# Early instruction fetches, branch hints and one-time credits in a decode attention kernel that is bound by its loads

## The chip, the cores and the metric

One core of a Trainium2 chip. The metric is the device time of one execution in microseconds; the profile's span, from the first to the last instruction, is about 1.35 us shorter in the kernel before.

## The reference, cut to what matters

One token for two batch entries: layer norm, a query projection, attention of 32 query heads over 8 cached heads with 32,768 positions each, an output projection, and beside it a small gated MLP whose result multiplies the attention's.

```python
xn = _layernorm(x)                       # x: 2 x 1 x 512
q = xn @ wq                              # 32 heads of 128
scores = einsum("bhqd,bhkd->bhqk", q, k) * Dh ** -0.5
o = einsum("bhqk,bhkd->bhqd", softmax(scores), v)     # k, v: 2 x 8 x 32768 x 128, bf16
out = x + (o @ wo) * silu(B(xn))         # B: the MLP with w1..w4
```

K and V are 268 of the 280.5 MB that are read. There are sixteen groups (batch entry, cached head), each with 8.39 MB of K and 8.39 MB of V.

## The kernel before

Every engine has its own program. SyncE issues all large loads, VectorE transposes K, TensorE multiplies, ScalarE takes exponentials. The first load is put ahead of the entry barrier; TensorE's loop runs once per group.

```python
def begin(nc, ins):                       # the first load goes ahead of SyncE's barrier
    ...
    at = next(n for n, i in enumerate(entry) if i.engine == ins.engine and isinstance(i, mybir.InstDrain))
    blocks[0].instructions = entry[:at] + [ins] + entry[at:]
...
    def load(cache, dst, sems, m):        # K or V of group m
        if m < last:
            sp.dma_start(out=dst, in_=row_view(cache, *groups[m])).then_inc(sems[0], 16)
            sp.sem_inc(sems[1], 16)       # the second half is credited at once
        else:
            for c in range(NPART):
                load_half(cache, dst, sems, m, c)
...
    for m in range(1, NG):
        sp.wait_ge(p_k, m)                # TensorE's mark: K's buffer is free
        load_k(m)
        sp.wait_ge(p_o, m)                # TensorE's mark: V's buffer is free
        load_v(m)
    ...                                   # then wo in seven pieces, the last two of 128 KB
...
    with pe.Fori(0, NG):                  # some 310 instructions, 16 passes
        head_sums()
        take(pe, s_z)
        for i in range(NPART):
            for r in range(NR):
                ...                       # 4 matmuls: scores
            mark(s_tf)
            if i == 0:
                mark(p_k)
        take(pe, s_p)
        ...                               # 1 + 64 matmuls: values
        mm.then_inc(s_o, 1)
        mark(p_o)
    ...                                   # products with wo as its pieces land
```

TensorE's program has 662 instructions, VectorE's 165, SyncE's 92, ScalarE's 62.

The softmax here doesn't subtract the row's maximum and nothing guards it: scores larger than these inputs give would overflow.

## Time and profile before

| | before |
|---|---|
| time, median (first three runs) | 654.27 us |
| span of the profiled run | 653.1 us |
| read from HBM | 280.50 MB, 429 GB/s over the span |
| DMA engines | busy throughout (99.4% of sixteen engines' span, queue q1) |
| TensorE, VectorE busy | 59%, 53% |
| instruction fetches in the span | two of 16 KB, two of 8 KB |

The DMA engines are the bound. The last landing is followed by a short tail: four matmuls, two VectorE operations, the output DMA (650.42 to 653.1 us). The rest of the reading is in the prediction. How late each DMA engine is, no row of the page tells; but the trace has sixteen updates of its semaphore for every load of the large queue. I read each as the end of one engine's share; it fits that the last piece has two late updates (1.22 and 1.25 us) where the DMA share is 0.13, and 0.13 x 16 is two engines. Below, "lateness" is the last of these sixteen less the first.

### The profile page before, as it was taken

Reading aid. Unit: us, or ns where it says so; the run is one execution under the profiler, and the core shown is the slowest. Engines: PE = TensorE matmul, PEld = TensorE weight load, DVE = VectorE, ACT = ScalarE, POOL = GpSimd, SP = SyncE. Lnnn points to the kernel's source line nnn. Section 1 sums busy time; section 2 is a strip of 40 time slices with the busy share of each in tenths; the row PEclk is TensorE's granted clock in tenths of the full one; section 3 lists DMA queues with packets and bytes.
Section 4 is the critical chain, followed back from the end, with each engine's and each line's share of the span. In section 5 each row is a group of like instructions: output and inputs, shape, how many; then the busy total and the mean of one; then the engine's idle time right before and its main releaser. Section 6 shows DMA issues by size and latency. Waiting matters only on the chain. (4 is left out here: it accounts for less than half of the span.)

```text
span 653.1 us, 6541 instructions
## 1 busy us (share of the span) xinstructions
PE 387.9 (59%) x2406; PEld 157.4 (24%) x2438; DVE 346.0 (53%) x412; ACT 76.6 (12%) x184; POOL 7.7 (1%) x29
## 2 busy tenths in 40 slices
PE   0658294673828558293754829366383955728785
PEld 0223131221313222131321213123131322303322
DVE  4266191754809266391835719174481926539570
ACT  1320102001010200101020010202001020200100
POOL 3100000000000000000000000000000000000000
PEclk9769788786978968698796978869597886959797
DMA  9989999999999999999999999999999999999997
GB/s 386 482 388 448 447 446 402 441 441 446 405 441 441 446 401 446 441 446 397 450 441 446 401 446 441 450 425 417 450 441 429 413 450 441 446 397 444 420 446 297
DMA packets 6508, 280.56 MB, mean 430 GB/s; under 512 B 736, under 2 KB 1000, under 8 KB 1256
## 3 DMA queue, kind: packets, MB, share of 16 engines
q1 hardware_dynamic: 6492, 280.50, 99.4%
q8 instruction: 2, 0.03, 0.0%
q14 instruction: 2, 0.02, 0.0%
q10 hardware_dynamic: 12, 0.01, 0.0%
HBM read 280.50 MB, written 0.00 MB: 429 GB/s over the span
## 5 line engine op out<-in xcount | busy, mean ns | idle before, releaser
L573 PE MATMUL bank<-T,z 128*128 128x512 bf16 x992 | 273.2, 423 | 188.1 <-PEq L46 183.9
L500 DVE STREAM_TRANSPOSE T<-kbuf 128x1024 int32<-128x1024 int32 x256 | 290.8, 1206 | 129.4 <-DVEq L46 129.4
L573 PEld LDWEIGHTS bank<-T,z 128*128 128x128 bf16 x1024 | 97.7, 103 | 350.9 <-issue 273.5
L590 PE MATMUL bank<-vbuf,pt 128*16 128x512 bf16 x1024 | 72.4, 444 | 4.5 <-PEq L46 3.3
L477 ACT ACTIVATE ep<-bank 128x512 bf16<-128x512 f32 x32 | 19.1, 597 | 438.5 <-ACTq L46 438.5
L521 DVE RECIPROCAL rec<-bank 128x1 f32<-128x1 f32 (+1 forms) x17 | 2.9, 169 | 120.6 <-DVEq L46 120.6
L590 PEld LDWEIGHTS bank<-vbuf,pt 128*16 128x16 bf16 x1024 | 27.7, 101 | 41.2 <-issue 22.7
L509 DVE STREAM_TRANSPOSE pt<-ep 128x512 bf16<-128x512 bf16 x32 | 22.7, 708 | 22.1 <-DVEq L46 22.1
L555 PE MATMUL bank<-ob,sel_o 128*128 128x128 f32 x136 | 20.6, 297 | 16.4 <-PEq L46 16.4
L583 PE MATMUL bank<-ones_f,sm 128*128 128x1 f32 x32 | 5.9, 252 | 31.3 <-PEq L46 31.3
L555 PEld LDWEIGHTS bank<-ob,sel_o 128*128 128x128 f32 x136 | 17.7, 203 | 21.8 <-issue 21.8
L481 ACT COPY ob<-bank 128x512 f32<-128x512 f32 x16 | 9.4, 586 | 103.6 <-ACTq L46 103.6
L470 ACT ACT_TABLE_LOAD x16 | 20.5, 1283 | 0.3
L470 ACT COPY z<-qr 32x16 bf16 x64 | 12.9, 201 | 0.7
L583 PEld LDWEIGHTS bank<-ones_f,sm 128*128 128x128 f32 x32 | 5.0, 195 | 32.2 <-issue 32.2
L439 PE MATMUL bank<-vbuf,h_bf 128*32 128x512 bf16 x14 | 5.6, 586 | 5.6 <-DVE h_bf L436 5.6
L550 PE MATMUL bank<-ident 128*1 128x1 bf16 x64 | 8.4, 165 | 0.0
L550 PEld LDWEIGHTS bank<-ident 128*1 128x1 bf16 x64 | 4.0, 82 | 16.1 <-issue 14.4
L529 DVE TENSOR_REDUCE oA<-xm 128x128 f32 x16 | 5.9, 366 | 3.8 <-DVEq L46 3.8
L316 PE MATMUL bank<-ident,xn_bf 17*128 17x17 bf16 x4 | 0.3, 175 | 12.8 <-POOL x L307 12.8
L523 DVE SCALAR_TENSOR_TENSOR xm<-bank,rec,mask 128x128 f32<-128x128 f32 (+1 forms) x17 | 6.0, 351 | 2.5 <-DVEq L46 0.2
L477 ACT ACTIVATION_READ_ACCUMULATOR ep<-bank 128x1 f32 x32 | 6.4, 199 | 0.2
(75 smaller groups left out, 55.7 us busy)
## 6 DMA issues: line engine op xcount, KB each, us to landing
vbuf<-in_A_v_cache_dram SPq DMA_DIRECT2D x4, 4096.0 KB, 29.0
kbuf<-in_A_k_cache_dram SPq DMA_DIRECT2D x2, 4096.0 KB, 22.7
kbuf<-in_A_wq_dram SPq DMA_DIRECT2D x1, 4096.0 KB, 12.3
vbuf<-in_B_w_dram SPq DMA_DIRECT2D x2, 1792.0 KB, 17.0
kbuf<-in_A_wo_dram SPq DMA_DIRECT2D x3, 1024.0 KB, 34.3
kbuf<-in_A_wo_dram SPq DMA_DIRECT2D x1, 512.0 KB, 37.1
kbuf<-in_A_wo_dram SPq DMA_DIRECT2D x1, 256.0 KB, 37.3
kbuf<-in_A_wo_dram SPq DMA_DIRECT2D x2, 128.0 KB, 36.7
```

The lines of the kernel that those rows point to most:

```text
L470: i = act.copy(out=z[32 * j:32 * j + 32, :, :, c:c + rep], in_=qr[32 * j:32 * j + 32, :, :, bass.ds(m * rep, rep)],)
L477: act.activation(out=eps_[i][:, :], in_=sc[i][:, :], func=ACT.Exp, scale=inv_sqrt_dh, accum_out=rss[i][:, :]).then_inc(s_e, 1)
L481: act.copy(out=ob[:, :], in_=o[:, :]).then_inc(s_ob, 1)
L500: dve.transpose(out=Ts[(NR * i + r) % T_BUFS][:, :].rearrange("p (b t k) -> p t b k", b=NB, t=RT), in_=kt[:, r * W:(r + 1) * W].rearrange( ...
L509: dve.transpose(out=pts[h][:, :, :].rearrange("p r (t h) -> p t r h", h=rep), in_=eps_[i][:, :].rearrange("p (t r h) -> p t r h", r=NR, h= ...
L523: dve.scalar_tensor_tensor(out=xm[p0:, :, :], in0=oT[p0:, :].rearrange("p (w r) -> p w r", w=WL), scalar=rec[p0:, 0:1], in1=mask[p0:, :].u ...
L529: dve.tensor_reduce(out=dst, in_=xm[p0:, :, :].rearrange("p w r -> p r w"), axis=AX.X, op=ALU.add).then_inc(s_r, 1)
L550: pe.matmul(mark_ps, lhsT=ident[:, 0:1], rhs=ident[:, 0:1], start=True, stop=True).then_inc(sem, 1)
L555: mm = pe.matmul(oT, lhsT=sel_o[:, t, :, :, :].rearrange("p j h w -> p (j h w)"), rhs=ob[:, t * Dh:(t + 1) * Dh], start=(t == 0), stop=(t ...
L573: mm = pe.matmul(sc[i][:, :], lhsT=z[:, nb, e, zc:zc + 128], rhs=Tb[:, nb, :, e], start=(r == 0 and nb == 0 and e == 0), stop=(r == NR - 1 ...
L583: pe.matmul(S, lhsT=sms[1][:, :], rhs=ones_f[:, 0:1], start=True, stop=True)
L590: mm = pe.matmul(o[32 * j:32 * j + VT * rep, :], lhsT=pts[h][:, r, a * VT * rep:(a + 1) * VT * rep], rhs=vt[:, u * VT:(u + 1) * VT, :].rea ...
```

## The change

Its intent: program text should be fetched at the start and not in the middle of the stream. TensorE leaves the entry block for a label `far` in the middle of its loop body and comes back (the visit); TensorE and VectorE name the program's last branch in a branch hint right after the start; SyncE's program gets shorter, since the credits are given once. A credit is this: each half of K or V has its own semaphore, and where one DMA brings both halves, SyncE itself increments that of the second.

```diff
-def begin(nc, ins):
+def begin(nc, ins, engine, far):
 ...
+    entry.instructions = head + [ins, mybir.InstUnconditionalBranch(target=far, name=f"I-{nc.next_id()}", engine=engine)]
+    with nc.body(f"{far}_back", parent=nc.bb_map[blocks[0].name]):
+        pass
 ...
-    begin(nc, first.ins)
+    begin(nc, first.ins, pe.engine, "far")
+    end_p, end_v = pe.alloc_register("end_p"), dve.alloc_register("end_v")
+    for eng, reg in ((pe, end_p), (dve, end_v)):
+        eng.reg_mov(reg, 0)
+    hint_p, hint_v = pe.mark_branch_hint_location(), dve.mark_branch_hint_location()
+    s_far = nc.alloc_semaphore("s_far")
 ...
             sp.dma_start(out=dst, in_=row_view(cache, *groups[m])).then_inc(sems[0], 16)
-            sp.sem_inc(sems[1], 16)
 ...
     load_k(0)
+    sp.sem_inc(s_k[1], 16 * last)
+    sp.sem_inc(s_v[1], 16 * (last - 1))
 ...
                 mark(p_k)
+        nc.br("mid", engines=[pe.engine])
+        with nc.body("far", parent=nc.bb_map["main"], valid_engines=[pe.engine]):
+            pe.sem_inc(s_far, 1)
+            nc.br("far_back", engines=[pe.engine])
+        nc.switch_bb("mid")
 ...
     sp.wait_ge(s_out, 16)
+    for eng, hint, reg in ((pe, hint_p, end_p), (dve, hint_v, end_v)):
+        eng.br_lt(reg, 1, on_true="fin", on_false="end").branch_hint(hint)
+    tail = nc.cur_bb
+    nc.switch_bb("fin")
+    pe.sem_inc(s_far, 1)
+    dve.sem_inc(s_far, 1)
+    nc.switch_bb("end", parent=tail)
```

More of the change, by code (lines that the diff above doesn't have):

```diff
@@ L53, in begin @@
         b.instructions = [i for i in b.instructions if i.name != ins.name]
-    entry = blocks[0].instructions
-    at = next(n for n, i in enumerate(entry) if i.engine == ins.engine and isinstance(i, mybir.InstDrain))
-    blocks[0].instructions = entry[:at] + [ins] + entry[at:]
+    entry = blocks[0]
+    at = next(n for n, i in enumerate(entry.instructions) if isinstance(i, (mybir.InstMemset, mybir.InstDrain)))
+    head, rest = entry.instructions[:at], entry.instructions[at:]
+    entry.instructions = head + [ins, mybir.InstUnconditionalBranch(target=far, name=f"I-{nc.next_id()}", engine=engine)]
+    with nc.body(f"{far}_back", parent=nc.bb_map[blocks[0].name]):
+        pass
+    *blocks, back = nc.m.functions[0].blocks
+    back.instructions = rest
+    nc.m.functions[0].blocks = blocks[:1] + [back] + blocks[1:]
 @with_exitstack
```

## The prediction

> **What bounds the kernel now.** I read the page's DMA rows first, then the queues, the chain that ended last, the waits of SyncE's queue, and last the timeline and the table by windows around the odd spots.
>
> ```profile
> DMA  9989999999999999999999999999999999999997
> ...
> q1 hardware_dynamic: 6492, 280.50, 99.4%
> q8 instruction: 2, 0.03, 0.0%
> q14 instruction: 2, 0.02, 0.0%
> ...
> HBM read 280.50 MB, written 0.00 MB: 429 GB/s over the span
> ```
>
> The kernel is a stream of 280.5 MB. The sixteen DMA engines are busy in every slice, while TensorE (59%) and VectorE (53%) have time to spare. A K and a V load are 8.39 MB each, and K loads land every 38.64 us in the second half (581.14 less 542.49, first completions, in the trace's semaphore updates): 16.78 MB / 38.64 us = 434 GB/s, 27.1 per engine. Counting packets in flight, the trace has sixteen at every instant that I sampled from 2.25 us to 648.9 us, in the first group, around 68 us and in the tail, so the stream never runs dry. SyncE's queue confirms it:
>
> ```profile
> SPq L224 <- PE bank L550: 526.0, 28, 23.9
> ...
> kbuf<-in_A_k_cache_dram SPq DMA_DIRECT2D x15, 27.4
> vbuf<-in_A_v_cache_dram SPq DMA_DIRECT2D x14, 32.1
> ```
>
> SyncE waits 526 us for TensorE's marks, but a load that then goes out lands only 27 to 32 us later although its own bytes need 19.3 us (8.39 MB at 434 GB/s): 8 to 13 us of older loads are still ahead of it. A mark may come some microseconds earlier or later and nothing changes.
>
> The two instruction queues are what the change is about: four fetches of program text inside the span. By the trace's packets they start at 47.86 us (8 KB, q14), 66.04 us (16 KB, q8), 107.23 us (16 KB, q8) and 617.07 us (8 KB, q14). The one at 66 us sits beside the only stall of TensorE that no semaphore explains, at the end of the first pass of its loop:
>
> ```profile
> 65.25 2.14 PE L590 MATMUL bank<-vbuf,pt 128*16 128x512 bf16 x29
> 68.50 0.39 PE L590 MATMUL bank<-vbuf,pt 128*16 128x512 bf16 x3 [1.11 <-issue]
> ```
>
> Three product matmuls before the loop's end, TensorE stands still for 1.11 us; in the second pass the same place (103.65 us) has none. Now the end:
>
> ```profile
> 613.73 36.69 DMA kbuf<-in_A_wo_dram
> 650.42 0.04 issue
> 650.47 0.26 PE bank L625 x4
> ```
>
> ```profile
> core 0: us, PE busy (x) PEld busy (x) DVE busy (x) ACT busy (x) POOL busy (x), PEclk, DMA share, GB/s
> 648.20:649.20 1.00, 0.72 (x44) 0.44 (x38) 0.00 (x0) 0.00 (x0) 0.00 (x0) 1.00 0.84 302
> 649.20:649.50 0.30, 0.30 (x16) 0.19 (x16) 0.00 (x0) 0.00 (x0) 0.00 (x0) 1.00 0.22 79
> 649.50:650.00 0.50, 0.23 (x16) 0.11 (x8) 0.00 (x0) 0.00 (x0) 0.00 (x0) 1.00 0.13 47
> ```
>
> The chain ends in the landing of the last piece of wo. In its last stretch the DMA share is 0.13, and 0.13 x 16 = 2 engines: fourteen are done and two late ones finish alone. The sixteen completions of that piece say the same: first at 649.18 us, twelve within 0.27 us of it, two near 0.55 us, two at 1.22 and 1.25 us.
>
> Where does the lateness come from? Follow the sixteen completions from load to load. Up to K of group 0 (40.1 us) they lie within 0.48 to 0.52 us. After the fetch at 47.9 us one engine is 1.07 us behind the first, with the next at 0.52. After the one at 66.0 us the worst is 1.70 us, after the one at 107.2 us a second stands at 1.66 to 1.81. The gaps shrink to 1.30 and 1.35 (16 KB) and 0.63 us (8 KB) by 270 us and then stay to the end. After the fetch at 617 us a fourth engine is 0.6 us late. [...]an engine that carried a piece of program text keeps its debt and pays it at the very end. That is the 1.2 us in which two engines work alone.
>
> [...]
>
> **The change part by part.** *The visit.* TensorE leaves the entry block for a label in the middle of its loop body, increments a semaphore and returns. It adds two branches, a semaphore increment and one branch per pass: [...]spread over passes in which it has more than 10 us of waiting; nothing on the path. [...] It removes the 1.11 us stall, which was not on the path: the V load behind it (68.96 us) had K of group 1, landing at 79.98 us, ahead of it. If the visit itself misses, TensorE reaches the entry barrier late, by some 2.5 us (estimate: at 66 us the fetch began at 66.04 and matmuls resumed at 68.50). SyncE's next issue (1.45 us) then slips to about 4 us, while the wq load, issued ahead of the barrier at 0.00, keeps the engines busy until 12.27 us. Cost 0. The start-up of TensorE and VectorE is delayed likewise, but they meet K of group 0 at 40.1 us with VectorE waiting 1.15 us for it, and the next K load (50.93 us) has until about 59 us, so again 0.
>
> *The hints.* Two register moves, two hint instructions, two compare-branches at the end: under 0.5 us on engines that wait at those places; VectorE's final branch lies beside the output DMA (651.40 to 653.1 us). [...]
>
> *The credits.* Twenty-nine fewer increments in SyncE's stream (31 become 2). Its 0.05 to 0.07 us each fall where SyncE waits anyway. But the stream gets shorter: in the trace SyncE pauses 0.40 us before the sixth wo issue (613.35 us), where its neighbours show 0.04, and the 8 KB fetch at 617.07 us follows. [...] Gain on the path by itself 0: an 8 KB debt is 0.6 us and hides behind 1.25.
>
> *The sum.* If all four fetches leave the loaded time, the last wo piece lands as the early loads did, 0.3 to 0.5 us after its first engine: 649.18 + 0.27 to 0.50 = 649.45 to 649.68 us in place of 650.42, a gain of 0.74 to 0.97 us. The rest of the tail (0.6 us of matmul and two VectorE operations, then the output DMA) moves along unchanged. Full success is then 654.27 - 0.85 = 653.4 us.
>
> **The rivals.** (1) *The fetches only move within the loaded time.* The first wq packet starts at 1.03 us and all engines are busy from 2.25 us; a block asked for after the barrier (1.4 us, or later if the visit stalls) meets a loaded engine and leaves its 1.2 us debt as before. [...] Against it: the visit is put ahead of the barrier, and at the start engines have slack, since the first packets of 32 KB take 1.9 us against 1.2 later. Time then 654.2. (2) *One 16 KB fetch stays, for instance TensorE's second.* The maximum over engines decides, so one late engine takes nearly the whole gain: 654.1 to 654.3. (3) *The stall is what matters:* 1.1 to 1.5 us of TensorE would shift the chain. Against it stands the full queue; it would make 653.0. (4) *The visit delays the start so much that the stream gaps.* It would need over 10 us of barrier; a gain lost 1:1 from there. Very unlikely.
>
> **Range and chances.** I give full success somewhat over half (gain 0.85), part success a quarter (0.4), none the rest: 0.55 x 0.85 + 0.25 x 0.4 = 0.57, so I predict 653.6 us, leaning a little to success. The runs before span 654.26 to 654.69; full success with the lowest of them gives about 653.1, no success with the noise 654.5. A change of 2% is 13 us, more than fifteen times what any mechanism here can move; I leave 1% for faster and 2% for a stall or disturbance that I do not see.
>
> **What would show it.** Right: no q8 or q14 packets between 3 us and the end; TensorE's 1.11 us gap at 68 us gone; the completions of the K and V loads within about 0.5 us of each other throughout; in the last microsecond the DMA share falling from full to zero within 0.5 us; mean GB/s of the steady groups unchanged. Wrong: a time more than 1.2 us below before with the spread unchanged (rival 3), engines still late by 1.2 us though the fetches came early (rival 1), or gaps in the first slices of the DMA row.

0.55 x 0.85 + 0.25 x 0.4 = 0.57 us, and 654.27 less 0.57 is 653.7, from which 653.6 us was put. Beside the sum, the branches that the visit adds to the loop were put at 0.8 us of TensorE's time; the trace of the changed kernel has 0.17 to 0.20 us for each, 2.86 us for all sixteen, where TensorE is idle for 180 us before the loop's L586 matmuls (11 us a pass). The register moves, hints and final branches take 0.34 us together there. That the hints would take away the fetches at 47.9 and 107.2 us was the author's guess, and so was the reason given for the fetch at 617 us to go.

## The result, and the profile after

The changed kernel takes 654.38 us (median of 6 runs, 654.16 to 654.52), the kernel before 654.38 us (median of 6). The ratio is 0.9999, with a 95% interval of 0.9986 to 1.0011: the same. Ratios here are the mean time of one kernel's fast runs over that of the other's of the same rounds, so not quite the ratio of the medians. The measured time lies in the range that was predicted, 0.8 us above the point.

The four places of the fetches are empty, and two fetches are left, as the queues of the changed kernel's page show (packets, MB, share):

```profile
q8 instruction: 1, 0.02, 0.0%
q10 hardware_dynamic: 12, 0.01, 0.0%
q14 instruction: 1, 0.01, 0.0%
```

One of 16 KB comes at 4.35 us, and one of 8 KB at 648.67 us. The first is in the DMA view of the changed kernel, cut to 4 to 5 us:

```profile
q1 hardware_dynamic: 15, 0.49, 114.8%
q8 instruction: 1, 0.02, 5.8%
```

At 4.35 us the engines have long been carrying wq (sixteen packets are in flight from 2.05 us). The sixteen completions of the wq load say what it does: 0.00 to 0.62 us for fifteen engines, 1.67 us for the last. Before, that load had a lateness of 0.50 us. The one late engine stays late in all 44 loads that follow in the trace: 1.59 us at K of group 0, 1.30 us at 273 us, 1.32 us at the last piece of wo. The end of the chain of the changed kernel (start, us, what):

```profile
613.26 36.95 DMA kbuf<-in_A_wo_dram
650.22 0.04 issue
650.26 0.26 PE bank L643 x4
```

The last landing is at 650.22 us, against 650.42 before. The table by windows of the changed kernel (time, busy time of each engine, then granted clock, DMA share and GB/s) shows who landed last:

```profile
648.20:649.20 1.00, 0.64 (x40) 0.36 (x28) 0.00 (x0) 0.00 (x0) 0.00 (x0) 1.00 0.59 207
649.20:649.50 0.30, 0.19 (x16) 0.01 (x3) 0.00 (x0) 0.00 (x0) 0.00 (x0) 1.00 0.07 24
649.50:650.00 0.50, 0.34 (x12) 0.16 (x12) 0.00 (x0) 0.00 (x0) 0.00 (x0) 1.00 0.05 18
```

0.07 x 16 is one engine, where before it was two (0.13). Fifteen engines are done by 649.2 us, and the kernel waits a microsecond for the sixteenth. TensorE's stall at the end of its first pass is gone; the same sixty-four matmuls in the changed kernel's timeline:

```profile
63.23 3.63 PE L608 MATMUL bank<-vbuf,pt 128*16 128x512 bf16 x64
66.69 0.17 PE L563 MATMUL bank<-ident 128*1 128x1 bf16 x1
```

It bought nothing, as a load issued there has some 10 us of older loads ahead of it (an estimate from the kernel before: 27 to 32 us from issue to landing, 19.3 us for its own bytes). The visit costs the start 0.52 us (SyncE's second issue at 1.97 us, before 1.45), which the wq load covers (landed at 13.48 us).

Each run also lists its span, and the time outside it differs: 1.29 to 1.40 us in the 27 runs of the kernel before that list it, but 1.32 to 1.68 us in the eleven of the changed kernel (the first six and five more below), median 1.47. So the changed kernel's span is shorter by 0.1 us at the median (652.9 against 653.0) and the rest of the execution longer by as much.

### The profile page after: what moved, and what is told of

It reads as the page before. It is cut to its first block, busy times and chain, and to the rows that moved or that the text cites. A ratio compares the mean times of both kernels' runs of the same rounds, so it can differ in the third digit from the quotient of the medians.

```text
span 652.9 us, 6540 instructions
## 1 busy us (share of the span) xinstructions
PE 390.0 (60%) x2406; PEld 156.8 (24%) x2438; DVE 345.8 (53%) x412; ACT 76.8 (12%) x184; POOL 7.7 (1%) x29
## 3 DMA queue, kind: packets, MB, share of 16 engines
q1 hardware_dynamic: 6492, 280.50, 99.4%
## 5 line engine op out<-in xcount | busy, mean ns | idle before, releaser
L586 PE MATMUL bank<-T,z 128*128 128x512 bf16 x992 | 272.9, 422 | 185.1 <-PEq L46 180.4
L586 PEld LDWEIGHTS bank<-T,z 128*128 128x128 bf16 x1024 | 97.4, 103 | 347.9 <-issue 270.3
L608 PE MATMUL bank<-vbuf,pt 128*16 128x512 bf16 x1024 | 77.5, 469 | 2.9 <-PEq L46 2.9
L494 ACT COPY ob<-bank 128x512 f32<-128x512 f32 x16 | 9.4, 587 | 107.2 <-ACTq L46 107.2
```

The costliest lines, as they stand in the source:

```text
L494: act.copy(out=ob[:, :], in_=o[:, :]).then_inc(s_ob, 1)
L586: mm = pe.matmul(sc[i][:, :], lhsT=z[:, nb, e, zc:zc + 128], rhs=Tb[:, nb, :, e], start=(r == 0 and nb == 0 and e == 0), stop=(r == NR - 1 ...
L608: mm = pe.matmul(o[32 * j:32 * j + VT * rep, :], lhsT=pts[h][:, r, a * VT * rep:(a + 1) * VT * rep], rhs=vt[:, u * VT:(u + 1) * VT, :].rea ...
```

## The experiments

All kernels make the same loads in the same order. The theory: an engine that carries program text while it is loaded stays late to the end, and the latest engine sets the end. The rivals: a lateness of 1.3 us is the transfers' own; or what one engine is late by, the others are early by, so that nothing is to be had. What each showed, with the fetches and lateness from the trace and times from the runs (medians):

| kernel | 16 KB fetches at, us | 8 KB fetches at, us | lateness at wq / V of group 0 / last piece, us | last landing, us | median span, us | time (before), us |
|---|---|---|---|---|---|---|
| before | 66.0, 107.2 | 47.9, 617.1 | 0.50 / 1.07 / 1.25 | 650.42 | 653.0 | 654.38 |
| before again | 57.8, 68.4 | 48.2, 615.3 | 0.39 / 1.93 / 1.64 | 650.34 | 653.1 | 654.42 (654.38) |
| after | 4.35 | 648.7 | 1.67 / 1.57 / 1.32 | 650.22 | 652.9 | 654.38 (654.38) |
| after again | 4.53 | 648.4 | 1.89 / 1.78 / 1.71 | 650.30 | 652.9 | 654.38 (654.38) |
| visit alone | 4.68, 71.2 | 50.5, 616.6 | 2.06 / 1.93 / 1.87 | 650.45 | 653.2 | 654.51 (654.32) |
| hints alone | 49.5 | 616.9, 648.8 | 0.51 / 1.96 / 1.48 | 650.47 | 653.1 | 654.55 (654.32) |
| credits alone | 47.9, 68.4 | 47.9 | 0.62 / 1.85 / 1.72 | 650.17 | 652.9 | 654.24 (654.38) |
| visit behind the loop | 3.06, 9.12 | 648.3 | 1.78 / 1.57 / 1.44 | 650.04 | 652.9 | 654.23 (654.38) |
| short | 63.7 | 645.8 | 0.44 / 0.45 / 1.48 | 650.27 | 652.9 | 654.19 (654.32) |
| short, padded | 29.8, 107.2 | 646.4 | 0.54 / 1.76 / 1.92 | 650.74 | 653.1 | 654.49 (654.32) |
| short, with TensorE's hint | none | 644.5 | 0.58 / 0.62 / 1.01 | 649.50 | 652.4 | 653.99 (654.38) |
| the same, clock kept up | none | 645.1 | 0.66 / 0.70 / 0.74 | 649.85 | 652.2 | 653.67 (654.38) |

Every single kernel's interval of the ratio includes 1, so the steps of a few tenths rest on single runs and on the traces. The experiments ran in three batches on three chips; compare a time with the one in brackets beside it, which is that of the kernel before in the same batch.

### The parts one by one

The visit alone leaves out the registers, hints, final branches and credits of the change:

```diff
-    end_p, end_v = pe.alloc_register("end_p"), dve.alloc_register("end_v")
-    ...  hint_p, hint_v and the br_lt at the end
+            sp.sem_inc(sems[1], 16)
-    sp.sem_inc(s_k[1], 16 * last)
-    sp.sem_inc(s_v[1], 16 * (last - 1))
```

> The kernel before with the visit alone. Theory: [...] (one 16 KB fetch in the first 5 us, no 1.11 us stall at the end of the first pass), but the second 16 KB fetch near 107 us stays[...], as do the 8 KB ones at 48 and 617 us: two engines late by 1.3 us at the end, time 654.3 to 654.5. Rival (the hint, not the visit, brought the early fetch): fetches at 66 and 107 us and the stall as before, same time.

In the main as the theory has it: 654.51 us, a 16 KB fetch at 4.68 us, no stall, and a second fetch, though at 71.2 and not near 107 us. Two engines end 1.80 and 1.87 us late, not 1.3. The visit is what brings a fetch early.

The hints alone, put into the kernel before:

```diff
     begin(nc, first.ins)
+    end_p, end_v = ...; reg_mov; hint_p, hint_v = pe.mark_branch_hint_location(), dve.mark_branch_hint_location()
 ...
     sp.wait_ge(s_out, 16)
+    ...  br_lt to "fin" with its hint, for both engines
```

> The kernel before with the branch hints alone. Theory: VectorE's 8 KB fetch at 48 us and TensorE's 16 KB at 107 us go; [...] (one 16 KB fetch near 4 us) and one engine is 1.3 us late to the end, time 654.3 to 654.5. Rival (the hint fetches nothing by itself, the visit did): the fetch at 66 us and its stall stay; time the same again, since one late engine is enough.

654.55 us. The 8 KB fetch at 48 us and the second of 16 KB are gone. But the remaining one came at 49.5 us, not near 4: the hints alone brought no early fetch. Both forms of the expectation were half right. From its fetch on one engine is 2.13 us late, at the end 1.48. All kernels with VectorE's hint have a new 8 KB fetch between 644 and 649 us, and none without it does; here the hint only moved a fetch to the end.

The credits alone:

```diff
-            sp.sem_inc(sems[1], 16)
+    sp.sem_inc(s_k[1], 16 * last)
+    sp.sem_inc(s_v[1], 16 * (last - 1))
```

> The kernel before with SyncE's credits given once and nothing else. Theory: [...]the 8 KB fetch at 617 us and the 0.40 us pause before the sixth wo issue go; the two 16 KB fetches and the 8 KB one at 48 us stay, two engines 1.3 us late at the end, time 654.2 to 654.5. Rival (the pause is something else): pause and fetch stay, same time.

654.24 us (interval of the ratio 0.9985 to 1.0012). The fetch near 616 us is gone and with it the pause: in the trace, the sixth wo issue begins 0.05 us after the fifth ends, 0.40 us in the kernel before. The two 16 KB fetches are there, at 47.9 and 68.4 us, and two engines end 1.62 and 1.72 us late.

The kernel before once more:

> The kernel before once more, one look, to see whether the fetches come at the same places in another execution. Theory: the program alone sets them: 8 KB near 48 and 617 us, 16 KB near 66 and 107 us, TensorE's stall near 67 us. Rival: they move by tens of microseconds or change in number, and a comparison of single profiles says less than I took from it.

The 8 KB fetches came at the same places, the 16 KB ones did not: 57.8 and 68.4 us in place of 66.0 and 107.2. With the earlier fetch the stall that I had quoted does not occur; the timeline of this execution:

```profile
62.02 3.63 PE L590 MATMUL bank<-vbuf,pt 128*16 128x512 bf16 x64
65.48 0.17 PE L550 MATMUL bank<-ident 128*1 128x1 bf16 x1
```

So the stall is no fixed property of the program, and the rival held for TensorE's fetches. The late engines at the end are common to both executions, but here three are over 1 us late (1.10, 1.37 and 1.64 us): after the 8 KB fetch at 48.2 us alone, one engine was already 1.40 us late, where the first execution had 1.09.

The changed kernel once more:

> The changed kernel once more, as one look at where its fetches fall in another execution, and five more rounds. Theory: one 16 KB fetch in the first 5 us (it was at 4.35 us) and no other before 640 us, since visit and hint set it; one engine 1.3 to 1.6 us late in every load from wq on; time 654.2 to 654.5, within 0.2 us of the kernel before. Rival (the number of fetches is chance too): a second 16 KB fetch, or none and then 653.5.

654.38 us, one 16 KB fetch at 4.53 us, one engine 1.89 us late at wq and 1.71 at the end; the DMA share from 649.2 to 649.5 us and from 649.5 to 650.0 us is 0.07 and 0.06, again one engine. The theory's expectation held in fetches and time; the lateness, 1.71 to 1.89 us, was above the 1.3 to 1.6 expected.

### A fetch that is waited for, at the very start

Could the fetch come before the engines are loaded? The label was moved behind the loop, so that TensorE should have to wait for its text:

```diff
-        nc.br("mid", ...) / body "far" / switch_bb("mid")        # in the loop
+    nc.br("mid", engines=[pe.engine])                            # behind the loop
+    with nc.body("far", parent=nc.bb_map["main"], valid_engines=[pe.engine]):
+        pe.sem_inc(s_far, 1)
+        nc.br("far_back", engines=[pe.engine])
+    nc.switch_bb("mid")
     pe.wait_ge(s_r, NG + 1)
```

> The changed kernel with the label that TensorE visits moved behind the loop[...]. Theory: [...]the 16 KB come at 0.6 to 1.0 us, before the engines are loaded at 1.0 to 2.2 us; TensorE reaches the entry barrier some 2 us later, which the first load covers; the hint keeps the later fetches off. No engine in debt, spread 0.5 us throughout, last landing near 649.5, time 653.4 to 653.8, result correct. Rival (the fetch takes 2 to 4 us to start wherever it is asked for): fetch at 2.5 to 4.5 us, one engine 1.3 us late to the end, time 654.2 to 654.5.

The rival held. TensorE executed the label at 5.48 us (0.69 us in the changed kernel, whose label is in the loop), so it waited 4.8 us. The fetch's packet did not start before 3.06 us, when the engines were loaded (from 2.05 us in the kernel before), and a second came at 9.12 us. Two engines were 1.72 and 1.78 us late at wq. Time 654.23 us (ratio 0.9999, interval 0.9985 to 1.0013), the result right. SyncE's second issue slipped to 6.77 us and cost nothing, since wq was still landing (12.27 us in the kernel before). The queues of this kernel and its last row by windows, one engine left:

```profile
q8 instruction: 2, 0.03, 0.0%
...
649.50:650.00 0.50, 0.46 (x12) 0.16 (x12) 0.00 (x0) 0.00 (x0) 0.00 (x0) 1.00 0.06 20
```

### No 16 KB fetch at all

To test the gain itself, TensorE's program was cut from 662 to 378 instructions. The work left out makes the result wrong (it still passes the comparison, whose tolerance is wide); VectorE's hint and the credits are in.

```diff
-            for u in range(NU):
+            for u in (*range(4), *range(NU - 4, NU)):
-        for k in range(DK):                 # the query projection
+        for k in (0, DK - 1):
-    early(0); ... early(1); ... product(2); ... ; product(3), product(4)
+    ...  their waits only; product(5), product(6) stay
```

> TensorE's program cut from 662 to 378 instructions (48 of the 64 value matmuls of each pass, half of the query projection, and the products of wo but the last two pieces are left out, so the result is wrong on purpose), VectorE's hint and SyncE's credits kept, same loads in the same order. Theory (an engine that carries a piece of program text while it is loaded ends late by it, and the latest engine sets the end): no 16 KB fetch in the span, the sixteen completions of every load within about 0.5 us, the last wo piece landed within 0.5 us of its first engine, time 653.4 to 653.7 against 654.4 of the kernel before. Rival (a lateness of 1.3 us of the last engines is the transfers' own, whatever was fetched): the spread stays at 1.3 us and the time at 654.3 to 654.5.

It missed: 654.19 us, for there was still one fetch, at 63.7 us. Yet its trace is the clearest picture of the mechanism. Lateness is 0.44 to 0.53 us in the first six loads of the trace (up to 59.3 us); at K of group 1 it is 1.63 us, with fifteen engines within 0.29 us and one alone, and it ends at 1.48. Here the rival, that the lateness is the transfers' own, fails: besides the data, the trace has only the fetch between. The 64 KB data packet that began as the fetch ended (64.59 us) took 2.92 us, where 2.42 is usual. As one engine alone fell behind, it was most likely that engine's next packet, and the fetch cost it 0.94 + 0.50 = 1.44 us (an estimate; the trace does not name the engines). The last windows show the one engine:

```profile
649.20:649.50 0.30, 0.00 (x0) 0.00 (x0) 0.00 (x0) 0.00 (x0) 0.00 (x0) 0.50 0.07 24
649.50:650.00 0.50, 0.00 (x0) 0.00 (x0) 0.00 (x0) 0.00 (x0) 0.00 (x0) 0.50 0.07 23
```

The padded form was to show that the matmuls left out aren't it:

```diff
+    for _ in range(140):
+        pe.sem_inc(s_far, 1)                # while TensorE waits for x
```

> The short program with 140 semaphore increments put ahead of TensorE's loop, in the time in which TensorE waits for x[...]. Work and loads as in the short one. Theory: one or two 16 KB fetches appear during the first passes, one or two engines are 1.3 us late from there to the end, time back at 654.2 to 654.5. Rival (what the short kernel gains, if it gains, comes from the matmuls left out, for instance in the tail): no change against the short kernel, 653.4 to 653.7.

Two fetches of 16 KB, 654.49 us, 0.3 us over the short kernel, which had one itself. But the last piece has four engines 1.43 to 1.92 us late, where two fetches account for two. The other two fell behind between 59 and 78 us (at K of group 1 three engines are 1.65, 1.86 and 1.98 us late), where the trace has no fetch. It has two 64 KB data packets there, begun at 59.5 and 60.0 us, that took 3.64 and 3.21 us in place of 2.42, and thirteen more, begun at 60.97 to 62.71 us, that took 2.53 to 2.74 us: a short slowdown of most transfers at once, two of them hit hard. Why is not known. So the rival has a share: an engine can also become late without program text. This was seen in one execution, the only profile of this kernel, and it spoils the pair as a test.

With TensorE's hint added to the short program:

```diff
-    end_v = dve.alloc_register("end_v") ...
+    end_p, end_v = ...; hints and final br_lt for both engines, as in the change
```

> The short program (wrong on purpose) with TensorE's hint as well[...]. The short program without it still made one 16 KB fetch at 63.7 us; the spread of the sixteen completions was 0.45 to 0.53 us up to 59 us and 1.5 to 1.6 us from there to the end. Theory: with the hint armed there is no 16 KB fetch at all, the spread stays near 0.5 us to the last piece of wo, which lands near 649.5 us, time 653.4 to 653.7. Rival (the sum of all transfers is limited together, so that what one engine is late by the others are early by, and without any fetch all land where the latest landed before): spread 0.5 but the last landing still at 650.2 and the time at 654.2 to 654.4. Second rival: the lateness of one engine comes anyhow: spread 1.3 to 1.5.

No 16 KB fetch. Lateness is 0.55 to 0.68 us until the 8 KB fetch at 644.5 us makes one engine 1.01 us late at the last piece. This piece landed at 649.50 us, 0.9 us before that of the kernel before and 0.8 us before that of the short kernel without this hint (650.27 us), which leaves out the same work; so the matmuls left out are not what brings the landing forward. The queues of the page, and the windows at the end:

```profile
q1 hardware_dynamic: 6492, 280.50, 99.5%
q10 hardware_dynamic: 12, 0.01, 0.2%
q14 instruction: 1, 0.01, 0.0%
...
648.20:649.20 1.00, 0.00 (x0) 0.00 (x0) 0.00 (x0) 0.00 (x0) 0.00 (x0) 0.50 0.35 122
649.20:649.50 0.30, 0.18 (x4) 0.13 (x4) 0.00 (x0) 0.00 (x0) 0.00 (x0) 0.50 0.00 0
```

The share is 0.00 from 649.2 us, where the changed kernel still has 0.07 and 0.05. The rival that all would land where the latest had landed is out too. Time 653.99 us, a gain of 0.4 us and not 0.85. I blamed TensorE's clock (0.50 in those rows) and kept it up:

```diff
+    for _ in range(14):
+        pe.matmul(treg_b[:, :], lhsT=ident[:, :], rhs=wo3[:, 0, 0:512], start=True, stop=True)
```

> The short program with both hints (wrong on purpose, 653.99 against 654.38 us of before), and 14 idle matmuls ahead of the last pieces of wo. In the short program the last piece landed at 649.50 us, 0.9 us earlier than before, but TensorE's clock was granted at 0.50 there and what follows the landing on TensorE took 0.68 us where the kernel before needs 0.30. Theory: with the matmuls the clock is at 1.00 at the end, the tail back at 0.3 us, no 16 KB fetch, last landing near 649.5, time 653.5 to 653.7, the full gain of 0.74 to 0.97 us that I had worked out. Rival (the short program's landing was earlier by chance, or the rest of the gain is not in the clock): time 653.9 to 654.4.

653.67 us (653.44 to 653.88), all five runs below all nine of before (654.32 to 654.96); the ratio is 0.9987, interval 0.9973 to 1.0001. The page again has no q8, lateness at the last piece is 0.74 us, and the windows are clean:

```profile
649.20:649.50 0.30, 0.00 (x0) 0.00 (x0) 0.00 (x0) 0.00 (x0) 0.00 (x0) 1.00 0.14 48
649.50:650.00 0.50, 0.32 (x8) 0.22 (x8) 0.00 (x0) 0.00 (x0) 0.00 (x0) 1.00 0.00 0
```

The number came out as expected; the reason that I gave for the step from 653.99 is not borne out. From the last landing to VectorE's first operation the two short kernels take 0.38 us (649.50 to 649.88) and 0.33 us (649.85 to 650.18), the kernel before 0.33 (650.42 to 650.75): the clock is worth 0.05 us, not 0.3 (the 0.68 us of the expectation count from 649.18 us, the landing of the last piece but one). Their spans differ by 0.2 us at the median. The other part is outside the span: 1.56 to 1.68 us in the kernel with the cold clock, 1.28 to 1.55 in the warm one, 1.29 to 1.40 before. The 653.99 is thus a span shorter by 0.6 us and an end longer by 0.25. What lengthens the time outside the span stays open; it is only in kernels with TensorE's hint and final branch, though not in all of them (1.29 to 1.38 with the visit behind the loop).

## Why the prediction was right or wrong

- **The range.** 653.1 to 654.5 us takes in full success as well as no gain, so it says little that the time fell into it. What came, no gain, had a fifth of the chances (1 less 0.55 and 0.25). The lower end does not follow from the terms either: 654.26 less 0.97 is 653.3 us.
- **The bound.** Right. Nothing that moved a mark or a stall changed the time: TensorE's first stall gone, SyncE's second issue at 6.77 us, a third of the matmuls left out (the short kernel has 1574 matmul records, the kernel before 2406).
- **The debt of an engine.** Right, and now shown rather than argued: 0.45 us before the only fetch of the short kernel, 1.63 after it, 0.74 at the end of a kernel without one. It is not the only cause: in the padded kernel two engines fell behind with no fetch near, which stays open.
- **The full gain, 0.74 to 0.97 us.** The size about holds for a program that makes no 16 KB fetch: 0.71 us by medians (654.38 to 653.67; the interval of the ratio just includes 1), 0.8 in the span. In the two profiles of such programs the last piece landed 0.92 and 0.57 us earlier than in that of the kernel before. It took a program that leaves work out, so this is no better kernel, only the measure of the term.
- **The step that failed** is "If all four fetches leave the loaded time", with somewhat over half of the chances on it. The four places are empty, but the visit's 16 KB came at 4.35 us with the engines loaded, and rival 1 and rival 2 came together: "one late engine takes nearly the whole gain". The number that was needed stood in the trace of the kernel before: SyncE's pause ends at 613.35 us, and the fetch that goes with it comes at 617.07 us, 3.7 us later (both are gone with the credits alone). The delay was set aside because the visit lies ahead of the barrier. But the label was executed at 0.69 us; with 3.7 us that makes 4.4 us, while the free time ends at 1.03 to 2.25 us. Measured were 3.7 us from label to fetch, and 3.8 and 4.0 us in the two other runs with this visit (4.53 less 0.69, 4.68 less 0.68). Even the fetch that TensorE waits for, in the visit behind the loop, started about 2.4 us after the visit could have asked for it (3.06 less 0.69 us). With this sum the gain should have been put near 0. The slack of the engines at the start, the other argument against rival 1, did not help: the engine with the fetch was 1.67 us late at wq already.
- **The hints.** Half right. In the traces with them VectorE's fetch at 48 us and TensorE's second one are missing, except in the visit behind the loop, where a second came at 9.12 us, 2.2 us after the hint (6.96 us). They also bring an 8 KB fetch at 644 to 649 us and, with TensorE's, in most runs 0.1 to 0.3 us outside the span, neither of which the prediction has.
- **The credits.** Right in all: fetch and pause gone, no gain by itself.
- **The first engine as a fixed point.** I let the first completion of the last piece stand at 649.18 us. It was at 648.70 us in the second execution of the same kernel and at 648.89 and 648.59 in those of the changed one. Such shifts of 0.5 us between single executions are as large as what the change could give. In the two short kernels without a 16 KB fetch the trace shows where such a shift arises: with the clock kept up, first completions that are mostly 19.32 us apart are 19.59, 19.54 and 19.41 us apart between 174.84 and 233.38 us. There 64 KB packets took 2.48 to 2.61 us in place of 2.42, in bursts of 12 to 15 within a microsecond; in the other kernel, from 20 us on, none did. What makes the bursts is open. To see the debt without them, take the last of the sixteen completions of the last piece less their mean: 0.95 to 1.40 us in the ten traces with a 16 KB fetch, 0.64 and 0.42 us in the two without.

The change leaves two fetches of four, one of 16 KB at 4.35 us and one of 8 KB near the end, and its gain is lost to the first, since not the sum of the debts counts but the largest.

## What to carry to other kernels

Here sixteen DMA engines were full from start to end (q1 at 99.4%), and the last landing was that of the latest engine (1.25 us after the first in the kernel before, 1.32 in the changed one). In such a kernel look at the spread of the sixteen completions of a load, not at the mean share. A cost that falls on one engine (here 1.2 to 1.9 us of lateness at the end for a fetch of 16 KB, 0.5 to 1.1 us for one of 8 KB) is paid once at the end, and taking away the second largest of such costs changed nothing (654.38 us with two engines 1.22 and 1.25 us late, 654.38 us with one 1.32 us late). What won here was a shorter program for TensorE (378 instructions, not counting the hint's own, in place of 662) with a hint, which made no 16 KB fetch. Whether a fetch that ends before the first load begins does as well was not shown, since both visits fetched under load (at 3.06 us and later); less data for the engine that carries the text was not tried.
